# A state-space scan and a bilinear feed-forward: warm-up products cut into narrow ones, and one up unit moved ahead of a pair's scores

## The chip, the cores and the metric

The kernel runs on one core of a Trainium2 chip. The metric is the device time of one execution in microseconds. A core has five engines that run side by side and meet through semaphores: TensorE (PE in the profile; its weight loads are listed apart as PEld), VectorE (DVE), ScalarE (ACT), GpSimd (POOL) and SyncE (SP). DMA transfers are issued from SP, ACT and POOL.

## The reference

The first half is a chunked state-space recurrence per batch (4) and head (8) over 768 tokens with head size 32 and state size 16. The second half multiplies two projections of its result and projects back.

```python
log_a = np.log(np.clip(a, 1e-06, 1.0))
for c in range(nc):                       # chunks of 32 tokens
    cum = np.cumsum(la, axis=-1)
    L = np.exp(cum[:, :, :, None] - cum[:, :, None, :]) * causal
    M = np.einsum('bhin,bhjn->bhij', Cc, Bc) * L
    y_intra = np.einsum('bhij,bhjd->bhid', M, xc)
    y_inter = np.einsum('bhin,bhnd->bhid', Cc, state) * np.exp(cum)[:, :, :, None]
    y[:, :, sl] = y_intra + y_inter
    Bx = np.einsum('bhjn,bhjd->bhjnd', Bc, xc) * decay_from_j[:, :, :, None, None]
    state = decay_full[:, :, None, None] * state + np.sum(Bx, axis=2)
...
x = attn_out.transpose(0, 2, 1, 3).reshape(3072, 256)
out = ((x @ w_a) * (x @ w_b)) @ w_out     # 256 -> 1536 -> 256
```

## The kernel before, in words

The sequence is cut into 6 blocks of 128 tokens. A *pair* is two batches of one block, so there are 12 pairs, two to a block; pairs 0 to 3 have one layout, later pairs another. All instructions stand in an order written out by hand; each engine runs its own in that order.

For a pair the work goes: B and C are scaled by running products of `a` (`scale_bc`), turned so that the state index lies on the partitions (`transposes` or, for later pairs, a transposing DMA, `turn`), multiplied into *scores* (`scores`, lines 428 and 443) in four PSUM banks `SC`, masked causally into SBUF (`mask`: line 483 on DVE; with `by_pool` a copy by ACT, line 480, and the product by POOL, line 481), and multiplied with x (`pv_u`, lines 489 and 503). `ds_mm` (lines 517 and 530) makes the pair's contribution to the state. x of a pair is scaled into `X16` by `scale_x` (line 318 on ACT, line 320 on POOL) or loaded as 16-bit.

The factors for the first two blocks come from PE too: DVE scans `a` (`scan`, line 262), inverts the middle value (`over_mid`) and spreads it (`sel_over_mid`, line 268); `factors_mm` (line 283) turns it with PE into `fps`; DVE's reciprocal (line 834) gives `fB`, and `scale_bc` (line 335) uses both.

The feed-forward of pairs 0 to 3 is made of *up units*. Unit (p, k2) makes two of twelve slices of the hidden layer for pair p: four products with Wa (`aps`, line 680), four with Wb (`bps`), ACT's copy of the first (line 707) and DVE's product of both (line 714). `go(...)` runs units one after the other. Twelve slices done, `out_half` (line 729) multiplies with Wo. From block 2 on both pairs go together (lines 759, 769, 784). `outputs`, called by `group`, makes the y of a block from scores, x and state. Their PSUM banks come from a list of digits, `BANKS`, taken in the order of the calls.

In front, PE has nothing to do until the first factors are there, and short waits after that. `warmup(n, bank, cols)` (line 255) fills them: n products of a zeroed tile with itself, 512 columns wide unless `cols` says otherwise, each with its own weight load, into a bank that nothing reads. They are ordinary instructions of PE's queue: what follows them starts behind them.

Weights are loaded by POOL's software queue in parts: `load_w0(0, 0)` (Wa, first half), `load_w0(1, 0)` and `load_w0(1, 1)` (two halves of Wb's first half), then `load_w`. On POOL these stand between computing instructions.

Of the kernel before, what the change touches and what calls it, by code (L numbers as in the profile page):

```python
# [28 lines left out]
def kernel(  # L29
# [82 lines left out]
    SC = [SC0[:, 0], SC0[:, 1], SC1[:, 0], SC1[:, 1]]  # L112
# [9 lines left out]
    def bank(name):  # L122
        return psf.tile([128, 512], f32, name=name, tag=f"ff{next(banks)}")
# [129 lines left out]
    def warmup(n, bank, cols=512):  # L253
        for _ in range(n):
            nc.tensor.matmul(  # L255
                bank[:, 0:cols], warm[:, 0:128], warm[:, 0:cols], start=True, stop=True, skip_group_check=True
            )


    def scan(lo, hi):  # L260
        for k in range(lo, hi):
            nc.vector.tensor_tensor_scan(Pr[:, k], a_sb[:, k], zero, 1.0, ALU.mult, ALU.add)
# [12 lines left out]
    def factors_mm(lo, hi, fps=None, k0=0):  # L275
        if fps is None:
            fps = bank("fps")
        w = 2 * NBP * H
        F = fps[:, k0 * w : (k0 + hi - lo) * w].rearrange("p (k r c) -> p k r c", k=hi - lo, r=2)
        for k in range(lo, hi):  # L280
            for r in range(2):
                for bt in range(2):
                    nc.tensor.matmul(  # L283
                        F[64 * bt : 64 * bt + 64, k - lo, r],
                        Pr[:, k].rearrange("p (i r) -> p r i", r=2)[:, r],
                        selr[:, k, bt],
                        start=True,
                        stop=True,
                        skip_group_check=True,
                        tile_position=(0, 64 * bt),  # L290
                    )
        return F.rearrange("p k r c -> p (k r c)")
# [14 lines left out]
    def flat(f, lo, hi):  # L307
        return f[:, lo:hi].rearrange("p k r b h -> p (k r b h)")
# [13 lines left out]
    def scale_bc(p, which, eng, factor=None):  # L322
        blk, bp = divmod(p, NBP)
        name, f = (("bm", fB), ("cm", fC))[which]
        raw = by_token(pair_in[p][which]) if p >= P0 else pair_in[p][which].rearrange("p h r n -> p r h n")
        if p >= P0 and which:
            eng.tensor_tensor(
                out=planes[p % 2][:, 4:6].rearrange("p t (h n) -> p t h n", n=N),
                in0=raw,
                in1=of_pair(f, blk, bp).unsqueeze(3).broadcast_to((128, 2, H, N)),  # L330
                op=ALU.mult,
            )
            return
        m_ = mid.tile([128, 2, H, N], f16, name=name, tag=name)
        eng.tensor_tensor(  # L335
            out=m_,
            in0=raw,
            in1=(of_pair(f, blk, bp) if factor is None else factor).unsqueeze(3).broadcast_to((128, 2, H, N)),
            op=ALU.mult,
        )  # L340
        st.setdefault(p, {})[name] = m_
        if p >= P0:
            dst = planes[p % 2][:, 0:4].rearrange("p (t e) (m f n) -> p t e m f n", e=2, f=2, n=N)
            for e in range(2):
                eng.tensor_copy(dst[:, :, e, :, e], m_.rearrange("p t (m f) n -> p t m f n", f=2)[:, :, :, e])
# [44 lines left out]
    def transposes1(which, T_):  # L390
        s = st[1]
        T_ = T_.bitcast(f16)[:, 0:256]
        for r in range(2):
            nc.tensor.transpose(
                T_[:, r * 128 : (r + 1) * 128],
                s[("bm", "cm")[which]][:, r].rearrange("p h n -> p (h n)"),
                ident,
            )
        if which:
            CT = mid.tile([128, 2, Q], f16, name="ct", tag="ct")  # L400
            nc.vector.tensor_copy(
                CT.rearrange("p t (i r) -> p r (t i)", r=2), T_.rearrange("p (r c) -> p r c", r=2)
            )
            s["CT"] = CT
        else:
            BT = mid.tile([128, 2, 2, 2, 64], f16, name="bt", tag="bt")
            s["BT"] = BT

            def part(e):
                nc.scalar.activation(  # L410
                    out=BT[:, e].rearrange("p r t i -> p (r t i)"), in_=T_, func=AF.Copy, scale=par[:, e : e + 1]
                )

            return part
# [7 lines left out]
    def scores(p):  # L422
        BT, CT = st[p]["BT"], st[p]["CT"]
        st[p]["T1"] = mid.tile([128, H, 2, Q], f16, name="t1", tag="t1")
        for e, bt, m in itertools.product(range(2), range(2), range(4)) if p >= P0 else ():
            rows = slice(32 * m, 32 * m + 32)
            c0 = (e * 2 + bt) * Q
            nc.tensor.matmul(  # L428
                SC[m][:, c0 : c0 + Q],
                BT[rows, e, bt],  # L430
                CT[rows, bt],
                start=True,
                stop=True,
                skip_group_check=True,
                tile_position=(32 * m, 0),
            )
        for e in range(2) if p < P0 else ():
            for r in range(2):
                for m in range(4):
                    for bt in range(2):  # L440
                        rows = slice(32 * m, 32 * m + 32)
                        c0 = (e * 2 + r) * Q
                        nc.tensor.matmul(  # L443
                            SC[m][64 * bt : 64 * bt + 64, c0 : c0 + Q],
                            BT[rows, e, r, bt],
                            CT[rows, bt],
                            start=True,
                            stop=True,
                            skip_group_check=True,
                            tile_position=(32 * m, 64 * bt),  # L450
                        )
# [13 lines left out]
    def product0(m2, e):  # L465

        return (
            st[0]["T1"][:, 4 * m2 : 4 * m2 + 4].rearrange("p (m e) r q -> p e m (r q)", e=2)[:, e],
            (SC0, SC1)[m2][:, :, e * 256 : e * 256 + 256],
        )  # L470

    def mask(out_in, by_pool=False, by_token=False):
        o_, i_ = out_in
        if by_token:
            c_ = causal_q.unsqueeze(1).broadcast_to((128, 4, Q))
        else:
            c_ = causal.rearrange("p r q -> p (r q)").unsqueeze(1).broadcast_to((128, 2, 2 * Q))
        if by_pool:
            tmp = mid.tile([128, *c_.shape[1:]], f32, name="tmp", tag="tmp")
            nc.scalar.copy(tmp, i_)  # L480
            nc.gpsimd.tensor_tensor(out=o_, in0=tmp, in1=c_, op=ALU.mult)  # L481
        else:
            nc.vector.tensor_tensor(out=o_, in0=i_, in1=c_, op=ALU.mult)  # L483
# [132 lines left out]
    def evac0(u, bt, eng, py):  # L616
        o_, i_ = X2T[:, 0, bt, u], py[bt][:, u * Q : (u + 1) * Q]
        if eng is nc.scalar:
            nc.scalar.activation(out=o_, in_=i_, func=AF.Copy, scale=YS)
        else:  # L620
            nc.vector.tensor_scalar(o_, i_, YS, None, ALU.mult)
# [96 lines left out]
    def unit(p, k2, between=None):  # L718
        a_ps = unit_mm(p, k2, Wa)
        if between:  # L720
            between()
        b_ps = unit_mm(p, k2, Wb)
        asb = evac_a(a_ps)
        return lambda: times(p, k2, b_ps, asb)
# [20 lines left out]
    def out_half(p, bt):  # L745
        o_ps = bank("ops")
        out_mm(p, bt, o_ps, range(NK))
        out_store(p, bt, o_ps)
# [68 lines left out]
    def go(*items):  # L817
        for p, k2 in items:
            unit(p, k2)()
# [2 lines left out]
        if ("S", p) in st:  # L822
            st[p].update(st.pop(("S", p)))

    warmup(26, SC[3], 128)
    scan(0, 1)
    over_mid(0, 1)
    sel_over_mid(0, 1, nc.vector)
# [3 lines left out]
    fps = bank("fps")  # L832
    v = factors_mm(0, 1, fps)
    nc.vector.reciprocal(flat(fB, 0, 1), v)
    warmup(1, SC[3])
    v1 = factors_mm(1, 2, bank("fps"))
    warmup(1, SC[3])
    scale_bc(0, 0, nc.vector)
    scale_bc(0, 1, nc.vector, v.rearrange("p (r b h) -> p r b h", r=2, b=NBP)[:, :, 0])
    scan(3, 4)  # L840
    tb, tcp = bank("tb"), bank("tc")
# [1 line left out]
    nc.scalar.copy(flat(fC, 0, 1), v)  # L843
    nc.scalar.copy(flat(fC, 1, 2), v1)
    scan(4, 5)
    warmup(1, SC[3])
    warmup(2, SC[3], 128)
    scores(0)
    scale_bc(1, 0, nc.gpsimd)
    mask(product0(0, 0))  # L850
# [1 line left out]
    mask(product0(1, 1), by_pool=True)  # L852
    scale_bc(1, 1, nc.vector)
    mask(product0(1, 0))
    warmup(3, tcp)
    part = transposes1(0, bank("tb"))
    part(0)
    part(1)
    warmup(2, tcp)
    py = [bank("py0"), bank("py1")]  # L860
    pv_u(0, 0, py, True)
    ds_mm(0, 256, py)
    transposes1(1, SC[0])
    for bt in range(2):
        evac0(0, bt, nc.scalar, py)
    warmup(1, tcp)
    pv_u(0, 1, py, True)
    for bt in range(2):
        evac0(1, bt, nc.scalar, py)
# [181 lines left out]
    prep(6)  # L1051
    masked(4, (0, 1, 2))
    out_half(2, 0)
    go((3, 0), (3, 1), (3, 2))
    scores(5)
    mask(product(5, 3), by_pool=True, by_token=True)
    prep_x(4)
# [3 lines left out]
    loads_bc(8)  # L1061
    masked(5, (0, 1, 2))
    out_half(2, 1)
    go((3, 3), (3, 4))
    scale_x(5, nc.scalar)
    go((3, 5))
    group(2)
# [92 lines left out]
```

## Time and profile before

| | |
|---|---|
| runs shown | 121.36, 121.40, 122.35 us; median 121.40 |
| profiled execution: time, span | 122.31 us, 120.6 us |
| PE busy | 114.6 us, 95% of the span |
| DVE, ACT, POOL busy | 87.2, 72.7, 62.3 us |
| warm-up products | 29 of 128 columns and 9 of 512, from 1.25 to 10.1 us |
| first product with factors (line 283) starts | 4.13 us |
| scores of pair 5 (line 428) start | 41.44 us |
| outputs of block 2, product with x (line 489) start | 46.05 us |

The times of a chain or timeline count from the span's start. A timeline line gives start, length, engine, line, operation, tile written and tiles read, shape and how many; in brackets the engine's idle time ahead of it and what ended it. In the chain of work that ended last, each piece is what held up the next; "issue" is time in which the engine waited for nothing that the profile shows.

### The profile page before, as it was taken

Reading aid. Unit: us, or ns where it says so; the run is one execution under the profiler, and the core shown is the slowest. Engines: PE = TensorE matmul, PEld = TensorE weight load, DVE = VectorE, ACT = ScalarE, POOL = GpSimd, SP = SyncE. Lnnn points to the kernel's source line nnn. Section 1 sums busy time; section 2 is a strip of 40 time slices with the busy share of each in tenths; the row PEclk is TensorE's granted clock in tenths of the full one; section 3 lists DMA queues with packets and bytes.
Section 4 is the critical chain, followed back from the end, with each engine's and each line's share of the span. In section 5 each row is a group of like instructions: output and inputs, shape, how many; then the busy total and the mean of one; then the engine's idle time right before and its main releaser. Section 6 shows DMA issues by size and latency. Waiting matters only on the chain.

```text
span 120.6 us, 3713 instructions
## 1 busy us (share of the span) xinstructions
PE 114.6 (95%) x1454; PEld 80.5 (67%) x1454; DVE 87.2 (72%) x171; ACT 72.7 (60%) x148; POOL 62.3 (52%) x109
## 2 busy tenths in 40 slices
PE   5998699999999999999999999999999999999990
PEld 5745499888898898645476464766464684655890
DVE  5989695995989888499984999677899445847100
ACT  0477557685965767787667737645646737566220
POOL 6998998299985686199912992249200000000200
PEclk9999999999999999999999999999999999999999
DMA  3999999997879999699588954879301012010032
GB/s 62 128 173 163 177 208 168 236 159 72 82 107 94 151 112 143 111 131 159 56 147 121 247 184 98 88 109 192 134 0 49 2 43 85 0 49 0 20 110 87
DMA packets 69185, 13.44 MB, mean 111 GB/s; under 512 B 64048, under 2 KB 68912, under 8 KB 69168
## 3 DMA queue, kind: packets, MB, share of 16 engines
q1 hardware_dynamic: 62272, 9.31, 47.5%
q0 software_dynamic: 4368, 3.54, 18.2%
q10 hardware_dynamic: 2528, 0.36, 2.1%
q8 instruction: 11, 0.18, 0.6%
q14 instruction: 6, 0.05, 0.1%
HBM read 11.11 MB, written 3.15 MB: 118 GB/s over the span
## 4 chain that ended last, share of the span: by engine, by line
PE 93%; DVE 3%; issue 1%; ACT 0%
PE ops L784 18%; PE aps L759 18%; PE bps L759 17%; PE ops L729 9%; PE bps L680 9%; PE aps L680 8%; PE SC L255 3%; PE SC L428 2%; PE SC L489 2%; PE SC L443 1%; DVE t L483 1%; PE SC L503 1%; PE aps L695 1%; PE SC L579 1%; PE fps L283 1%
## 5 line engine op out<-in xcount | busy, mean ns | idle before, releaser
L707 ACT COPY asb<-aps 128x512 f32<-128x512 f32 x72 | 41.6, 587 | 13.3 <-PE aps L759 9.6
L769 DVE TENSOR_TENSOR hkb<-bps,asb 128x512 f16<-128x512 f32 x48 | 32.3, 689 | 12.7 <-ACT asb L707 11.6
L759 PE MATMUL aps<-XB,Wa 128*128 128x512 f16 x96 | 28.6, 379 | 0.0
L759 PE MATMUL bps<-XB,Wb 128*128 128x512 f16 x96 | 28.5, 379 | 0.0
L784 PE MATMUL ops<-Wo,hkb 128*128 128x256 f16 (+1 forms) x204 | 22.5, 267 | 0.0
L784 PEld LDWEIGHTS <-hkb 128*128 128x128 f16 x204 | 18.5, 98 | 3.1
L483 DVE TENSOR_TENSOR t<-SC,causal_q 128x512 f16<-128x512 f32 x27 | 17.2, 682 | 3.3 <-PE SC L428 3.3
L714 DVE TENSOR_TENSOR hk<-bps,asb 128x512 f16<-128x512 f32 x24 | 16.1, 684 | 3.1 <-PE bps L680 1.2
L759 PEld LDWEIGHTS <-Wb 128*128 128x128 f16 x96 | 9.9, 103 | 10.9
L759 PEld LDWEIGHTS <-Wa 128*128 128x128 f16 x96 | 9.7, 103 | 9.1 <-issue 0.2
L798 POOL DMA_DIRECT2D out_dram<-osb x1 | 0.6, 642 | 27.9 <-ACT osb L796 27.9
L796 ACT ACTIVATE osb<-ops 128x256 f32<-128x256 f32 (+1 forms) x16 | 6.0, 377 | 14.3 <-PE ops L784 14.2
L680 PE MATMUL bps<-X2T,Wb 128*128 128x256 f16 x96 | 13.8, 273 | 0.0
L680 PE MATMUL aps<-X2T,Wa 128*128 128x256 f16 x88 | 12.7, 273 | 0.0
L729 PE MATMUL ops<-Wo,hk 128*128 128x256 f16 x96 | 11.5, 273 | 0.0
L481 POOL TENSOR_TENSOR t<-tmp,causal_q 128x512 f16<-128x512 f32 x5 | 5.8, 1159 | 10.0 <-ACT tmp L480 9.9
L680 PEld LDWEIGHTS <-Wb 128*128 128x128 f16 x96 | 9.8, 103 | 0.7
L729 PEld LDWEIGHTS <-hk 128*128 128x128 f16 x96 | 8.9, 98 | 1.4
L680 PEld LDWEIGHTS <-Wa 128*128 128x128 f16 x88 | 8.9, 103 | 0.6
L320 POOL TENSOR_SCALAR x<-xn 128x512 f16<-128x512 f32 x6 | 8.9, 1491 | 0.6
L483 DVE TENSOR_TENSOR t<-SC,causal 128x512 f16<-128x512 f32 x12 | 7.7, 683 | 0.8 <-PE SC L443 0.7
L335 POOL TENSOR_TENSOR bm<-bn,fB 128x256 f16<-128x256 f32 x11 | 6.9, 623 | 2.5 <-DMA bn<-in_B_dram 2.3
(115 smaller groups left out, 127.8 us busy)
## 6 DMA issues: line engine op xcount, KB each, us to landing
out_dram<-osb SPq DMA_DIRECT2D x22, 128.0 KB, 1.8
xn<-in_x_dram SPq DMA_DIRECT2D x6, 256.0 KB, 4.3
cn<-in_C_dram SPq DMA_DIRECT2D x8, 128.0 KB, 3.9
bn<-in_B_dram SPq DMA_DIRECT2D x8, 128.0 KB, 4.5
Wa<-in_moe_w_a_dram POOLq DMA_DIRECT2D x2, 384.0 KB, 6.4
Wo<-in_moe_w_out_dram POOLq DMA_DIRECT2D x2, 384.0 KB, 5.5
xn<-in_x_dram SPq DMA_DIRECT2D x4, 128.0 KB, 3.7
Wb<-in_moe_w_b_dram POOLq DMA_DIRECT2D x2, 192.0 KB, 6.1
```

The lines of the kernel that those rows point to most:

```text
L320: eng.tensor_scalar(xo, xi, XS, None, ALU.mult)
L335: eng.tensor_tensor(out=m_, in0=raw, in1=(of_pair(f, blk, bp) if factor is None else factor).unsqueeze(3).broadcast_to((128, 2, H, N)), op ...
L481: nc.gpsimd.tensor_tensor(out=o_, in0=tmp, in1=c_, op=ALU.mult)
L483: nc.vector.tensor_tensor(out=o_, in0=i_, in1=c_, op=ALU.mult)
L680: nc.tensor.matmul(ps[:, kk * 2 * Q : (kk + 1) * 2 * Q], w_of(W, k, f), X2T[:, p, :, f], start=(f == 0), stop=(f == 1), skip_group_check=True,
L707: (nc.vector.tensor_copy if on_dve else nc.scalar.copy)(asb, a_ps)
L714: nc.vector.tensor_tensor(out=s["hk"][:, 2 * k2 : 2 * k2 + 2, :].rearrange("p k q -> p (k q)"), in0=b_ps, in1=asb, op=ALU.mult)
L729: nc.tensor.matmul(o_ps[:, 0:d_model], hk[:, k, bt * Q : (bt + 1) * Q], Wo[:, k, :], start=(k == 0), stop=(k == NK - 1), skip_group_check= ...
L759: nc.tensor.matmul(t_, w_of(W, k, f), XB[:, blk - P0 // NBP, f].rearrange("p t j q -> p (t j q)"), start=(f == 0), stop=(f == 1), skip_gro ...
L769: return lambda: nc.vector.tensor_tensor(out=s["hk"][:, k], in0=ps[1], in1=asb, op=ALU.mult)
L784: nc.tensor.matmul(o_ps[:, 0:w], hk[:, k, c * Q : (c + 1) * Q], Wo[:, k, cs], start=(k == 0), stop=(k == NK - 1), skip_group_check=True,)
L796: nc.scalar.activation(out=o_sb[:, 0:w], in_=o_ps[:, 0:w], func=AF.Copy, scale=1.0 / (YS * YS))
```

## The change

The first call of `warmup` makes 34 narrow products in place of 26. Every later one of 512 columns is replaced by four of 128: the two between the factors' products, the one ahead of pair 0's scores, the three and the two around the transposes of pair 1, and the one ahead of `pv_u(0, 1)`. That makes 35 more products with 35 more weight loads, all ahead of the first up unit. Later, up unit (3, 3) moves ahead of the scores of pair 5, past `prep_x(4)`, `loads_x(6)`, `prep(7)`, `loads_x(7)`, `loads_bc(8)`, the masks of pair 5 and `out_half(2, 1)`. The list of banks stays, so unit (3, 3) now takes banks 1 and 3 and `out_half(2, 1)` takes bank 2, where they had 3 and 2, and 1.

```diff
-    warmup(26, SC[3], 128)
+    warmup(34, SC[3], 128)
     scan(0, 1)
...
     nc.vector.reciprocal(flat(fB, 0, 1), v)
-    warmup(1, SC[3])
+    warmup(4, SC[3], 128)
     v1 = factors_mm(1, 2, bank("fps"))
-    warmup(1, SC[3])
+    warmup(4, SC[3], 128)
     scale_bc(0, 0, nc.vector)
...
     scan(4, 5)
-    warmup(1, SC[3])
-    warmup(2, SC[3], 128)
+    warmup(6, SC[3], 128)
     scores(0)
...
     mask(product0(1, 0))
-    warmup(3, tcp)
+    warmup(12, tcp, 128)
     part = transposes1(0, bank("tb"))
     part(0)
     part(1)
-    warmup(2, tcp)
+    warmup(8, tcp, 128)
     py = [bank("py0"), bank("py1")]
     pv_u(0, 0, py, True)
     ds_mm(0, 256, py)
     transposes1(1, SC[0])
     for bt in range(2):
         evac0(0, bt, nc.scalar, py)
-    warmup(1, tcp)
+    warmup(4, tcp, 128)
     pv_u(0, 1, py, True)
...
     out_half(2, 0)
-    go((3, 0), (3, 1), (3, 2))
+    go((3, 0), (3, 1), (3, 2), (3, 3))
     scores(5)
     mask(product(5, 3), by_pool=True, by_token=True)
     prep_x(4)
...
     masked(5, (0, 1, 2))
     out_half(2, 1)
-    go((3, 3), (3, 4))
+    go((3, 4))
     scale_x(5, nc.scalar)
```

## The prediction

> **What bounds the kernel now.** I read the engine shares first, then the chain that ended last in order of time, then the engines' timelines in the two stretches that the change touches.
>
> ```profile
> PE 114.6 (95%) x1454; PEld 80.5 (67%) x1454; DVE 87.2 (72%) x171; ACT 72.7 (60%) x148; POOL 62.3 (52%) x109
> ...
> q8 instruction: 11, 0.18, 0.6%
> ...
> PE 93%; DVE 3%; issue 1%; ACT 0%
> ```
>
> TensorE (PE) carries 93% of the chain. From 14.77 us on the chain is PE work without a gap worth naming up to the last output, so a microsecond that PE loses anywhere is a microsecond at the end. All that can be won or hidden lies in the first 14.77 us:
>
> ```profile
> 1.25 2.95 PE SC L255 x26
> 4.21 0.54 PE fps L283 x8
> 4.75 0.54 PE SC L255
> 5.29 0.37 PE fps L283 x8
> ...
> 6.82 0.60 PE SC L443 x32
> ...
> 13.06 0.34 PE SC L503 x30
> 13.40 1.08 issue
> 14.48 0.21 PE SC L503
> 14.77 0.83 PE bps L680 x6
> ```
>
> The first product that the kernel needs, the factors of line 283, stands directly behind the 26 warm-up products: no wait lies between. Its operand had been ready on VectorE (DVE) since 3.54 + 0.18 = 3.72 us, and DVE then waits for it:
>
> ```profile
> 3.54 0.18 DVE L268 TENSOR_TENSOR selr<-sel,rmid 32x32 f32<-32x32 f32 x1
> ...
> 4.79 0.36 DVE L834 RECIPROCAL fB<-fps 128x32 f32<-128x32 f32 x1 [0.16 <-PE fps L283]
> 5.18 0.42 DVE L335 TENSOR_TENSOR bm<-bn,fB 128x256 f16<-128x256 f32 x1
> ```
>
> The second place is "issue" at 13.40: PE stands for 1.08 us in the middle of the 32 products of line 503, with no semaphore to wait for. The DMA records name a cause: queue q8, kind "instruction", moves 11 packets of 16 KB, one for about every 250 rows of PE (a row is a weight load or a product), so it is PE's code. The first runs from 12.28 to 13.23 us and PE goes on at 14.48, after 449 rows. I take it that the code ran out there.
>
> **The change, part by part.**
>
> *Wide into narrow.* Nine products of 512 columns become 36 of 128. The price per column is the same, by the starts in the trace: while the clock is still slow a narrow one follows the last after 0.107 us (26 in a row) and a wide one takes 0.43; later narrow ones (and the transposes of line 357, each with a weight load of its own) come every 0.055 us and wide ones every 0.216. Four narrow are 0.43 and 0.22 us, so nothing. What hides it if that is wrong: all of them but the first 34 stand ahead of a wait for DVE or POOL. The tightest is after the scores of pair 0: 12 narrow, two transposes, 8 narrow are 22 x 0.055 = 1.2 us, and the masks that the next products wait for come 1.4 us after these scores. That cover is 0.2 us.
>
> ```profile
> L255 PEld LDWEIGHTS <-warm x38: 95/147/147, 1.2 to 9.7; 128*128 128x128 f16 x38
> L255 PE MATMUL SC<-warm x32: 219/311/607, 1.3 to 6.4; 128*128 128x128 f16 x29, 128*128 128x512 f16 x3
> ```
>
> [...] The trace shows 55 ns and 216 here.
>
> *Eight more at the head.* They come before anything is due, and at the slow rate: 8 x 0.107 = 0.85 us. The clock opens at 5.31 us in the trace's clock record (the 512-column product at 4.68 lasts 607 ns, the one at 5.58 390), so the first factors, now at 4.13 + 0.85 = 4.98, run their second half faster: I take 0.1 off, 0.75. Bounds: all eight at the fast rate 0.44, all slow 0.85. What is late next: the reciprocal (4.79 to 5.54), bm, cm, the transposes, ct, the scores (6.82 to 7.57), the masks, all one dependency after the other on DVE, PE and ScalarE (ACT); the scan between them fills DVE but is shorter than the waits. On POOL the scaling of pair 1 (7.41, behind DMA issues that do not move) stays; the mask after it waits for the scores and moves by 0.7, and with it the issue of the second half of Wb's first part, 9.21 to 9.9. Its landing at 14.72 stays: the software queue is still moving the loads issued before it until 12.7, with the engines full.
>
> *What of the 0.75 is left at 14.77.* In this profile PE stands from 13.40 to 14.48 anyway, so a plain delay would vanish in it. But the 35 added products are 70 rows of code. If the code ends after 449 rows as before, that is now 70 rows earlier in the work: in the third of the six products of line 680 that began at 12.24, with five products and nearly all of line 503 still to do. PE gets there at 12.35 + 0.75 = 13.1 and stands until the code comes. If that is at 14.48 again (the packet waited on full DMA engines, whose traffic does not depend on PE), 5 x 0.109 + 0.2 for line 503 + 0.28 up to line 680 give 15.5 for 14.76: +0.75. Bounds: the request moves with the row that causes it; those rows are now about 1.0 us earlier (the row 256 before the stop ran at 8.80; now at 7.03 + 0.75), so the code is there at 13.5, PE comes to line 680 at 14.5 and waits for the landing at 14.72: nothing to +0.25. In the other direction the request comes later by the front's 0.6: +1.35. I take +0.75; the first packet started 3.5 us after the row 256 rows before the stop, the second only 2.2, which says that full DMA engines and not the row set it.
>
> *The up unit of pair 3.* Two evacuations, one product and 8 matmuls change places with the scores of pair 5; the work is the same, the scores come 4 x 2 x 0.109 = 0.87 us later, and with them ACT's copy and POOL's mask, behind which X of pair 4 is scaled:
>
> ```profile
> 42.63 1.16 POOL L481 TENSOR_TENSOR t<-tmp,causal_q 128x512 f16<-128x512 f32 x1 [1.46 <-ACT tmp L480]
> 43.88 1.50 POOL L320 TENSOR_SCALAR x<-xn 128x512 f16<-128x512 f32 x1
> ...
> 46.05 0.63 PE L489 MATMUL SC<-t,x 128*32 128x128 f16 x32
> ```
>
> That scaling ends at 45.38 and is wanted at 46.05: slack 0.67. It will end at 46.25, so PE waits 0.2, with the hop 0.25. Bounds 0 and 0.3. DVE's three masks end at 45.1 (44.21 before) and free the scores' banks for 45.81: hidden by 0.7; without that cover, their rest would be added. The banks of the products rotate in another order, but each one's last reader ends ahead of its next writer by 0.3 us or more. Behind on POOL stands the preparation of pair 7: its bm waits for a landing at 46.54 anyway, so its turn on SP's queue (47.89) and the loads of X of pair 7 and of pair 8's inputs behind it move by 0.3; the scores of pair 7 want them at 54.3. Nothing there.
>
> **The sum.** +0.75 + 0.25 = +1.0 us. The profiled execution has a span of 120.6 and a time of 122.31, so it becomes 123.3. The runs shown are 121.36, 121.40 and 122.35: the profiled one is like the third, 0.9 over the median. I add the sum to the median and round up a little, because a run without the stop at 13.40 has nothing to absorb the delay: 122.5 (own range 122.0 to 123.2).
>
> **The rivals.**
>
> *The stop is new or longer* (0.16). The quick runs may be those whose code comes in time, 0.9 us faster. Then 70 rows more make them stand too: 0.9 + 0.75 + 0.25 = +1.9, 123.3. For it: the two levels of times differ by about the stop. Against: one profile, and nothing that shows a quick run.
>
> *Narrow products come no faster than their weight loads* (0.08). The load's row says 95 to 98 ns in the fast state. At that rate the 22 take 2.1 us, 0.7 past the cover: +1.7, 123.1. Against: four in a row at 55 ns. [...]
>
> *The stop swallows the delay* (0.13). The code request moves up with its row, PE meets the landing of Wb at 14.72: +0 to 0.25, with pair 3's 0.25 +0.4: 121.8.
>
> *The stop disappears: no loss* (0.10). Place: 13.40. If the code is asked for so much earlier that it is there by 13.1, and the half of Wb without that packet in its way lands by 14.4 (its other fifteen engines were done at 13.57), PE reaches line 680 at 13.40 + 0.28 + 0.75 = 14.43 for 14.76: -0.33 + 0.25 = -0.1, 121.3. It decides from a resumption before 13.1, 1.4 earlier than now; the row moves by 1.0 only. If X of pair 4 is in time too, -0.3. More than 1% faster would need the eight products hidden, and the chain shows nothing that hides them.
>
> **How the numbers follow.** One per cent, 1.2 us, is about what a measurement of this kernel tells from no change. The forecast has 0.53: its upper part, over 122.6, is half, 0.26. With the two slower rivals, 0.24, slower has 0.50. Same has the forecast's lower half and the swallowed and vanished ones but for 0.07 that I leave for faster: 0.43. The range goes from the swallowed case's lower end, 121.5, to the new stop's upper end, 123.5.
>
> **What would show it.** Right: 34 narrow products at 0.107 us, line 283 at about 5.0, the reciprocal at 5.55, scores near 7.6; an idle "issue" of 1 us or more inside line 680 or its neighbours near 13.1 and none in line 503; line 680's second half of Wb at 15.5; line 489 at 46.3 counted from the same shift, behind POOL's line 320. Wrong: line 283 before 4.8, a gap that has gone, or line 680 at 14.8.

## The result and the profile after

The changed kernel takes 123.25 us (median of 21 runs, 122.59 to 124.67); the kernel before, in the same study, 122.43 (21 runs, 121.36 to 123.71). The ratio is 1.009, with an interval of 1.0066 to 1.0114. Measured once more, beside the second group of experiments (e8 below), it was 1.004 (1.0004 to 1.0076). So the change costs about 0.5 to 1.1 us by the two ratios. The ratios leave out executions that took over 1.5% more than the fastest of their kernel, and the medians and means here do not, so the two can differ by a few tenths of a per cent. The profiled execution took 124.22 us with a span of 122.5, 1.9 more than the one before; that is a worse draw than the median.

The page after, in the lines that answer to those of before (engine shares; code packets; the chain's shares):

```profile
PE 116.9 (95%) x1489; PEld 83.9 (68%) x1489; DVE 87.1 (71%) x171; ACT 72.7 (59%) x148; POOL 62.4 (51%) x109
...
q8 instruction: 11, 0.18, 0.6%
...
PE 73%; POOL 6%; DVE 5%; DMA 4%; SPq 4%; issue 3%; ACT 1%; POOLq 0%; DVEq 0%; ACTq 0%
```

PE has 35 products more. Its share of the chain has fallen from 93% to 73%: the end is now set in part by POOL, by a load (`cn<-in_C_dram`) and by SP's queue, which before were nowhere in it. The chain's head, in order of time:

```profile
1.25 3.81 PE SC L255 x34
5.06 0.54 PE fps L283 x8
5.60 0.54 PE SC L255 x4
...
8.39 0.66 PE SC L443 x20
...
14.03 0.66 PE bps L680 x6
14.69 0.35 PE SC L503 x32
```

Line 283 starts 0.85 us later, four narrow products take 0.54 us where one wide one took 0.54, and all 32 products of line 503 run in one piece: the "issue" of 1.08 us is gone. Here are the longest waits of PE over the whole span, after (in us, times, longest):

```profile
PE SC L255 <- DVE warm L202: 1.2, 1, 1.2
PE SC L503 <- POOL t L481: 1.0, 1, 1.0
PE SC L394 <- DVE cm L335: 0.2, 1, 0.2
PE SC L489 <- POOL x L320: 0.2, 1, 0.2
```

The second line is new. It is not in the front: it is pair 3, at 35.6 to 36.6 us, and the timeline of POOL shows where it comes from (the bracket is the idle time ahead and what ended it):

```profile
32.92 0.62 POOL L327 TENSOR_TENSOR planes<-cn,fC 128x256 f16<-128x256 f32 x1 [1.60 <-DMA cn<-in_C_dram]
33.50 0.62 POOL L335 TENSOR_TENSOR bm<-bn,fB 128x256 f16<-128x256 f32 x1
...
35.39 1.15 POOL L481 TENSOR_TENSOR t<-tmp,causal 128x512 f16<-128x512 f32 x1
```

POOL stands 1.60 us for pair 4's C. Behind that in its queue is `mask(product(3, 3))`, line 481, and PE's line 503 needs it: 35.26 + 0.35 us of work, then 0.98 idle up to 36.59. In the first profile of before, the same preparation began at 30.40 without a wait, the mask stood ready in time, and line 503 ran in one piece:

```profile
30.40 0.62 POOL L327 TENSOR_TENSOR planes<-cn,fC 128x256 f16<-128x256 f32 x1
...
32.88 1.16 POOL L481 TENSOR_TENSOR t<-tmp,causal 128x512 f16<-128x512 f32 x1
```

```profile
34.70 0.42 PE L503 MATMUL SC<-t,x 64*32 64x128 f16 x32
```

### The profile page after: what moved, and what is told of

Its sections match the earlier page's. It is cut to its first block, busy times and chain, and to the rows that moved or that the text cites. A ratio compares the mean times of both kernels' runs of the same rounds, so it can differ in the third digit from the quotient of the medians.

```text
span 122.5 us, 3783 instructions
## 1 busy us (share of the span) xinstructions
PE 116.9 (95%) x1489; PEld 83.9 (68%) x1489; DVE 87.1 (71%) x171; ACT 72.7 (59%) x148; POOL 62.4 (51%) x109
## 4 chain that ended last, share of the span: by engine, by line
PE 73%; POOL 6%; DVE 5%; DMA 4%; SPq 4%; issue 3%; ACT 1%; POOLq 0%; DVEq 0%; ACTq 0%
PE ops L784 18%; PE aps L759 17%; PE bps L759 17%; PE SC L255 5%; DMA cn<-in_C_dram 4%; SPq L143 4%; PE aps L680 4%; PE bps L680 3%; DVE t L483 3%; PE ops L729 2%; PE SC L489 2%; POOL t L481 2%; PE SC L428 2%; DVE hk L714 1%; POOL x L320 1%
## 5 line engine op out<-in xcount | busy, mean ns | idle before, releaser
L327 POOL TENSOR_TENSOR planes<-cn,fC 128x256 f16<-128x256 f32 x8 | 5.0, 621 | 7.3 <-DMA cn<-in_C_dram 7.3
```

## How the profiles are compared

Every experiment was timed and one execution of it profiled. From the scores of pair 6 (49.46 us before) on all profiles run alike within 0.02 us, so the differences in span can be split by the start times of a few products. For each profile these are set against the first profile of before, and the growth between one and the next is written down. *Front*: up to line 695. *Stop*: from there to the seventh product of line 680 with Wb (14.76 us before), where the code stop and the landing of Wb lie. *Pair 2*: to its scores (23.64); where it grows, PE waits for POOL's cm in line 357, and in m3, e6, e8 and m2 for Wb's next part in line 680 as well. *Pair 3*: to the scores of pair 4 (37.07), where the new wait lies. *Unit*: from line 579 to line 489 (46.05). *Pair 6*: to its scores (49.46), which wait for `turned` (in e5, by the profile, for ACT's copy of line 741). The rest is below 0.03 except 0.37 in n3, before the scores of pair 5. "Clock" is the time at which the clock record shows TensorE's full clock (e8 and m2 have no such entry; there the spacing of the warm-up products falls from 0.107 to 0.056 us at 4.6 and at 9.9 us); "rows" is the number of PE instructions (weight loads and products) that stand ahead of the first up unit more than before.

| profile | rows | clock | front | stop | pair 2 | pair 3 | unit | pair 6 | span |
|---|---|---|---|---|---|---|---|---|---|
| before, first | 0 | 5.31 | 0 | 0 | 0 | 0 | 0 | 0 | 120.61 |
| before, second (n4) | 0 | 5.29 | +0.12 | -0.93 | 0.00 | +0.04 | 0.00 | +1.03 | 120.85 |
| e3 unit alone | 0 | 8.89 | +0.77 | -0.27 | 0.00 | 0.00 | +0.25 | 0.00 | 121.35 |
| e2 eight alone | 16 | 5.85 | +0.78 | -0.39 | 0.00 | +0.21 | 0.00 | +0.34 | 121.54 |
| e7 eight and unit | 16 | 4.51 | +0.38 | -0.98 | 0.00 | 0.00 | +0.25 | 0.00 | 120.27 |
| m3 tiny eight | 16 | 9.63 | +1.09 | -1.27 | +0.70 | 0.00 | 0.00 | +0.40 | 121.50 |
| n3 tiny eight, loads early | 16 | 10.17 | +1.23 | -1.07 | +0.03 | 0.00 | 0.00 | +0.86 | 122.02 |
| n1 few rows | 22 | 5.36 | +0.72 | -0.91 | +0.32 | 0.00 | +0.25 | +0.35 | 121.32 |
| e1 narrow alone | 54 | 9.91 | +0.94 | -1.26 | +0.22 | +1.03 | 0.00 | +0.81 | 122.33 |
| e6 narrow and unit | 54 | 9.90 | +0.94 | -1.12 | +0.64 | +0.36 | +0.25 | 0.00 | 121.66 |
| e5 front | 70 | 4.21 | +0.24 | -0.93 | +0.20 | +0.39 | 0.00 | +0.50 | 120.99 |
| after, first | 70 | 9.82 | +1.63 | -1.27 | +0.20 | +1.11 | +0.25 | 0.00 | 122.52 |
| after, again (e8) | 70 | none shown | +0.42 | -0.80 | +0.50 | +0.71 | +0.25 | 0.00 | 121.68 |
| m1 rows, wide products | 70 | 4.71 | +0.57 | -0.76 | 0.00 | 0.00 | +0.25 | 0.00 | 120.67 |
| n2 the same again | 70 | 9.95 | +1.81 | -1.27 | +0.20 | +0.77 | +0.25 | 0.00 | 122.36 |
| e4 weights early | 70 | 10.03 | +2.06 | -1.26 | +0.17 | +0.64 | +0.25 | 0.00 | 122.45 |
| m4 loads early | 70 | 6.02 | +0.83 | -0.74 | 0.00 | 0.00 | +0.25 | 0.00 | 120.93 |
| m2 mask first | 70 | none shown | +1.63 | -1.27 | +0.70 | +1.42 | +0.25 | +0.33 | 123.64 |

Two things are plain before any single experiment. The times of one and the same kernel scatter by over 2 us (before: 121.4 to 123.7 in 21 runs), and a profile is one draw from that: the clock opens anywhere from 4.2 to 10.2 us. And the gains and losses are small waits in several places, not one delay that is carried through.

## Experiments

The theory first held against the result was the prediction's own (a delay of the front, carried through a stop that stays). The first group takes the change apart; "means" below are means of all timed runs, minus those of before in the same study, each with a standard error of about 0.25 us.

### Narrowing alone (e1)

Every call of 512 columns as in the change; the first warm-up keeps its 26 products.

```diff
-    warmup(1, SC[3])
+    warmup(4, SC[3], 128)
...
-    warmup(3, tcp)
+    warmup(12, tcp, 128)
...
```

> The narrowing alone: 26 products at the head, nine wide ones become 36 narrow, units in the old order. Theory 1 (the loss is made by the eight more at the head, which make POOL issue the weight loads late, and by the unit's move): the same within 0.3%, line 283 at 4.1 us, no wait of PE in line 503 of pair 3. Theory 2 (narrow products let TensorE's clock open later, 9.8 us in place of 5.3): most of the loss, 0.6 to 0.9%, the clock's opening after 8 us, the first scores 0.5 us or more late.

Measured: 122.68 us, ratio 0.9989 (0.9947 to 1.0031). Line 283 starts at 4.13 us as before, which it must, since nothing ahead of it was narrowed; between the two factors four narrow products took the time of the wide one. The stop is gone; the wait in pair 3 is there, 0.91 us.

### Eight more alone, wide products kept (e2)

```diff
-    warmup(26, SC[3], 128)
+    warmup(34, SC[3], 128)
```

> Eight more narrow products at the head alone, the wide ones stay. Theory 1: line 283 at 5.0, POOL's weight loads (line 176) issued 0.8 us or more late, pair 4's C landing late, PE waits 0.5 to 1 us in line 503 of pair 3 for POOL's mask: 0.5 to 0.8% slower. Theory 2: within 0.3%, since the delay goes into the stop at 13.4 us.

Measured: 122.92 us, ratio 0.998 (0.9939 to 1.0022). The front is 0.78 later and 0.39 of that is given back where the stop was: PE waits 0.81 for Wb's landing instead of 1.08 for code. In pair 3, POOL waits 0.80 us for pair 4's B, whose last parts land together at 32.2 us, and PE waits 0.09 for t.

### The unit's move alone (e3)

```diff
-    go((3, 0), (3, 1), (3, 2))
+    go((3, 0), (3, 1), (3, 2), (3, 3))
     scores(5)
...
-    go((3, 3), (3, 4))
+    go((3, 4))
```

> The unit's move alone. Both theories: PE waits 0.2 us ahead of line 489 for POOL's scaling of x of pair 4 (line 320), 0.25 us in all, 0.2% slower; the front as before. If the move is neutral, that wait is missing.

Measured: 122.72 us, ratio 0.9968 (0.9926 to 1.0011). The 0.25 us before line 489 is there, and in every profile with the move, and in none without. The stop is there too; PE's timeline:

```profile
13.77 0.41 PE L503 MATMUL SC<-t,x 64*32 64x128 f16 x30
15.04 0.23 PE L503 MATMUL SC<-t,x 64*32 64x128 f16 x2 [0.87 <-issue]
```

The front is 0.77 late although nothing in it differs from before: its clock opened at 8.89 us. So a clock can open late without narrow products.

### Weights issued earlier in the changed kernel (e4)

A rival for pair 3: POOL issues the weights later because its queue waits for a mask (10.84 us for 9.21), SP's loads behind them come later, and so does pair 4's C.

```diff
     scale_bc(1, 0, nc.gpsimd)
     mask(product0(0, 0))
     mask(product0(0, 1))
+    load_w0(1, 1)
+    w1 = load_w(1)
     mask(product0(1, 1), by_pool=True)
...
-    load_w0(1, 1)
-    w1 = load_w(1)
```

> The changed kernel, with the issues of Wb's second half, and of the second halves of Wa and Wb, ahead of POOL's mask of pair 0 in place of behind it. Theory 1: weights issued near 8 us, SP's loads of pair 3 start by 18.8 as in the kernel before, C of pair 4 lands by 30.5, the wait of 1 us in line 503 of pair 3 is gone: 0.1 to 0.4% over before. Theory 2: as the changed kernel, 0.9% over before.

Measured: 123.63 us, ratio 1.0072 (1.0029 to 1.0114). The weights are issued at 7.95 to 9.39 us and pair 3's B at 17.72 (20.01 in the changed kernel, 18.75 before), but pair 4's B still lands at 33.27 and PE still waits 0.36 us. Late weights are not the cause, at most a part of its size. Nor does the time at which the load is issued decide it: pair 4's C left at 22.66 us here, with a wait of 0.36 us, and at 27.03 in e2, with 0.09.

### The front of the change, without the unit's move (e5)

The edits of e1 and e2 together, which is all of the change but the unit:

```diff
-    warmup(26, SC[3], 128)
+    warmup(34, SC[3], 128)
...
-    warmup(1, SC[3])
+    warmup(4, SC[3], 128)
...
```

> The whole front of the changed kernel, units in the old order. If the parts simply add (theory 1): the eight carry it, 0.5 to 0.8% over before, no wait ahead of line 489. If the front's delay goes into the stop for code (theory 2): within 0.3% of before.

Measured: 122.98 us, ratio 1.002 (0.9981 to 1.0059). With the clock open at 4.21 us the 70 rows delay line 695 by 0.24 only. The wait in pair 3 stays, 0.26 us: it doesn't need a late front. And a short stop is left, in line 680:

```profile
12.48 0.27 PE L680 MATMUL bps<-X2T,Wb 128*128 128x256 f16 x1
12.94 0.71 PE L680 MATMUL bps<-X2T,Wb 128*128 128x256 f16 x5 [0.18 <-issue]
```

It stands behind 222 products and 223 weight loads, as the stops in line 503 of before and e3 do: 70 rows more in front have moved it to an instruction 70 rows earlier in the work.

### Narrowing and the unit; eight and the unit; the change again (e6, e7, e8)

e6 has the edits of e1 and e3, e7 those of e2 and e3, e8 is the changed kernel as it is. Against the changed kernel that is, for e6 and for e7 in turn:

```diff
-    warmup(34, SC[3], 128)
+    warmup(26, SC[3], 128)
```

```diff
-    warmup(4, SC[3], 128)
+    warmup(1, SC[3])
...
```

> The changed kernel with 26 products at the head. Theory 1: 0.2% over before, the wait of 0.2 us ahead of line 489, line 283 at 4.1. Theory 2 (the narrow ones and their code carry the loss): 0.6% or more.

> Eight more and the unit's move, wide products kept. Theory 1: as the changed kernel, 0.7 to 1.0% over before. Theory 2: 0.2%, the unit's move alone.

> The changed kernel once more, beside the same runs of before as the three parts. 0.7 to 1.1% over before. If TensorE's clock opens by chance early or late (it opened at 5.3, 5.9 and 8.9 us in runs with wide products, at 9.8 to 10.0 in three with narrow ones), this look may open at another time; if the narrow products hold it back, it opens after 9.5 again.

Measured: e6 122.87 us, 1.0043 (0.9999 to 1.0087); e7 123.06, 1.0022 (0.9983 to 1.0061); e8 123.38, 1.004 (1.0004 to 1.0076). The wait in pair 3: 0.24, none, 0.59 us. With all eight combinations the means can be averaged: with the eight minus without, +0.3 us; narrowing +0.3; the unit +0.15, each with a standard error of some 0.15 to 0.2. That they add up to the change's +0.8 fits several small costs; it doesn't prove any one of them.

Up to here the wait in pair 3 stood in all six profiles with the narrowing, 0.24 to 0.98 us, and in none of the four without it was it over 0.09. What differs at that place is a transfer. The landings of pair 4's B come in sixteen parts; in the six, fifteen are done and one is over a microsecond late, and the 16 KB code packet (queue q8) runs at that time. In the changed kernel the packet runs at 30.79 to 31.75 us, B's fifteenth part lands at 31.95 and the last at 33.34; in the first profile of before the packet comes at 32.06, after B's landing at 30.45. The packets follow the rows, plainest where they are far apart: the seventh and eighth begin after 1717 and 1973 rows before and after 1714 and 1977 in the changed kernel. So more rows ahead bring them earlier in the work.

### Wide products, and as many rows (m1, n2)

If rows do it, 70 rows without a narrow product must do it as well. Against the kernel before:

```diff
+    def tiny(n):
+        for _ in range(n):
+            nc.tensor.matmul(
+                SC[3][0:32, 0:32], warm[:, 0:32], warm[:, 0:32], start=True, stop=True, skip_group_check=True
+            )
+
+    tiny(35)
     warmup(26, SC[3], 128)
...
-    go((3, 0), (3, 1), (3, 2))
+    go((3, 0), (3, 1), (3, 2), (3, 3))
...
```

> The unit's move as in the change, but the wide products stay wide; instead of the narrowing and the eight more, 35 tiny products (32 weights x 32 columns) run at the very start: 70 more instructions in TensorE's stream, as in the change, at about the same time. Theory of the shifted code packets: the stop at row 449 is gone, the fourth 16 KB instruction packet runs at 29.5 to 31.5 us (before 32.06), pair 4's C and B land with a last engine 1 us or more behind, and PE waits 0.2 to 1.0 us for t of line 481 before line 503 of pair 3, with not one product narrowed: ratio 1.004 to 1.008. Theory that the narrow form itself makes that wait (other clock, other times of the front): packets as in the kernels with wide products or the wait absent, ratio 0.998 to 1.002.

> The kernel of wide products with 35 tiny ones ahead, once more. If the collision of the code packet with pair 4's landing is a matter of rows and of chance within it, a second look has a landing whose last engine is 1 us late and a wait before line 503 of pair 3; if wide products are spared, there is none, as in the first look. Ratio as before, 1.002 to 1.008.

Measured: m1 123.43 us, ratio 1.0043 (1.0007 to 1.0078); n2, the same kernel, 123.63, 1.0095 (1.0057 to 1.0133). The 35 cost about what the eight did: line 283 at 4.98 us in m1, 5.18 in n2. The first profile missed the expectation: packet at 29.45 us, B's last part only 0.25 us behind the others, no wait; the clock opened early in it, at 4.71 us, and C was issued at 25.36. The second, with the clock at 9.95 and C at 27.69, has it, packet at 30.58, B's last part 0.92 us behind at 33.18. PE and POOL in n2:

```profile
35.44 0.35 PE L503 MATMUL SC<-t,x 64*32 64x128 f16 x20
36.44 0.29 PE L503 MATMUL SC<-t,x 64*32 64x128 f16 x12 [0.64 <-POOL t L481]
```

```profile
33.34 0.62 POOL L335 TENSOR_TENSOR bm<-bn,fB 128x256 f16<-128x256 f32 x1 [1.19 <-DMA bn<-in_B_dram]
...
35.23 1.16 POOL L481 TENSOR_TENSOR t<-tmp,causal 128x512 f16<-128x512 f32 x1
```

So the narrow form is not needed for this wait, and with the rows it is frequent and not certain. In m1 the stop of the front is again left, 0.33 us at 13.42, in line 680 behind 222 products.

### Narrow products, and few rows (n1)

The counterpart: the first warm-up's columns in wide products, everything else as changed, 22 rows more than before in place of 70.

```diff
-    warmup(34, SC[3], 128)
+    warmup(8, SC[3])
+    warmup(2, SC[3], 128)
```

> The changed kernel, but its first warm-up of 34 narrow products is issued as 8 wide and 2 narrow ones: the same columns, 48 instructions less in TensorE's stream, so 22 more than before in place of 70; the other 38 narrow products and the unit's move stay. If the number of instructions ahead places the fourth code packet on pair 4's landing, it runs after it here (at 31 us or later), the last engine of B's landing is at most 0.3 us late, and PE doesn't wait for t before line 503 of pair 3: ratio 1.000 to 1.005. If the narrow form does it some other way, the wait of 0.25 to 1 us is there: ratio 1.004 to 1.010. Either way the stop at row 449 is gone and the unit costs 0.25 us before line 489.

Measured: 123.31 us, ratio 1.0082 (1.0038 to 1.0126). The fourth packet is back at 32.66 us, B lands whole at 31.17, and the wait in pair 3 is gone with 38 products still narrow:

```profile
34.83 0.42 PE L503 MATMUL SC<-t,x 64*32 64x128 f16 x32
```

```profile
31.33 0.62 POOL L335 TENSOR_TENSOR bm<-bn,fB 128x256 f16<-128x256 f32 x1 [0.18 <-DMA bn<-in_B_dram]
...
33.22 1.16 POOL L481 TENSOR_TENSOR t<-tmp,causal 128x512 f16<-128x512 f32 x1
```

The landing and the wait came out as expected. The time did not: the ratio is above the range given. In the profile, 0.25 us of the 0.71 is the unit, 0.35 a wait of pair 6, 0.32 lies in pair 2, and front and stop together give 0.19 back. Taking the wait in pair 3 away by this edit did not make the kernel measurably faster.

### Pair 4's loads earlier in the changed kernel (m4)

```diff
-    loads_x(3, nc.sync)
     loads_bc(4)
+    loads_x(3, nc.sync)
```

> The changed kernel, but SP issues pair 4's C and B ahead of pair 3's x, whose values are needed later. Theory that pair 4's landing collides with the code packet at 29.4 to 31.8 us: C and B are issued 1 to 4 us earlier, land before the packet, POOL's line 335 of pair 4 begins earlier and the wait before line 503 of pair 3 falls below 0.1 us; ratio 1.002 to 1.005. Theory that POOL is late for its own work (state sums, masks), not for the landing: wait unchanged, 0.25 to 1 us, ratio 1.006 to 1.010.

Measured: 123.03 us, ratio 1.0024 (0.9987 to 1.006). C is issued at 22.32 us (27.55 in the changed kernel), POOL's bm of pair 4 begins at 31.06 instead of 33.50, and the wait before line 503 is gone. Of the versions that keep all rows and the unit's move (the changed kernel, e4, m2, m4) this has the lowest ratio; its profile has 0.32 us left over before, 0.25 of it the unit's. It is not faster than before. Its front has a stop as well:

```profile
13.71 0.71 PE L680 MATMUL bps<-X2T,Wb 128*128 128x256 f16 x5 [0.36 <-issue]
```

### POOL's mask ahead of pair 4's preparation (m2)

```diff
 scores(3)
+mask(product(3, 3), by_pool=True)
 prep(4, (2,))
-mask(product(3, 3), by_pool=True)
```

> The changed kernel, but POOL's mask of pair 3 stands ahead of pair 4's preparation in POOL's queue. Theory of POOL's queue: the wait before line 503 of pair 3 is gone even though pair 4's C and B land late, the time falls by 0.25 to 0.6 us against the changed kernel, ratio 1.001 to 1.005; line 418 (turn of pair 4) starts at most 0.5 us later than it did and nothing waits for it. Theory that the loss sits in the front (a later clock, a later line 695): the wait goes but the scores of pair 4 and 5 are no earlier, ratio 1.007 to 1.010.

Measured: 125.06 us, ratio 1.0146 (1.0104 to 1.0188): a miss, 2 us over before. The wait before line 503 is gone, but POOL now sits out line 480 first (mask at 33.24 us) and begins the preparation of pair 4 at 34.36 where the changed kernel did at 32.92; its turn comes later and PE waits there instead:

```profile
PE SC L428 <- DMA turned<-planes: 1.6, 2, 1.4
```

POOL's queue is tight on both sides of this mask. Moving the mask ahead trades the wait in pair 3 for a larger one; an earlier landing (m4) takes it away.

### Sixteen rows more and nothing else; with the loads early as well (m3, n3)

These ask whether the saving at the stop can be had for less than it costs.

Against the kernel before, with `tiny` as above; n3 has m4's edit besides.

```diff
+    tiny(8)
     warmup(26, SC[3], 128)
```

> The kernel before with 8 tiny products (32x32, 16 more instructions) ahead of the first warm-up and nothing else. Theory that the stop is a matter of where the code packet is asked for: the stop of 1.08 us at row 449 is gone as with the eight products of 128 columns, the tiny products cost 0.1 to 0.4 us, no wait in pair 3: 0.3 to 0.9 us faster than before, ratio 0.993 to 0.998. Rival, that the stop is only moved or that the time of the front and not the rows takes it away: stop of 0.5 to 1.1 us still there, ratio 1.000 to 1.003.

> The kernel before with 8 tiny products (32x32) ahead of the first warm-up, and pair 4's C and B issued ahead of pair 3's x. If what the change pays is the landing of pair 4 and what it saves is the stop, this has the saving without the price: no stop, no wait in pair 3, no wait before line 489, 0.2 to 0.8 us faster than before, ratio 0.993 to 0.998. If both are small beside the time at which the clock opens, ratio 0.998 to 1.002.

Measured: m3 122.82 us, ratio 0.9994 (0.9959 to 1.0028); n3 123.14, 1.0052 (1.0012 to 1.0092). The stop is gone in both, and neither is faster. Both profiles have a late clock (9.63 and 10.17 us) and a front 1.09 and 1.23 us late, which eats most of the saving. n3 has waits for `turned` of 0.31 us in pair 5, the 0.37 left out of the table's columns, and 0.80 in pair 6 (its span is 122.02). In it the fourth packet (32.69 to 33.76 us) runs beside pair 5's C and B, whose last parts land 1.46 and 1.29 us behind the others; whether that makes the wait in pair 5 was not followed. No version that was run beats the kernel before beyond its interval.

### A second profile of the kernel before (n4)

> The kernel before once more, for its profile alone. If the stop belongs to the place of row 449 in the code, it is there again with 0.8 to 1.1 us, wherever the clock opens; if the first look had it by chance, TensorE waits there less than 0.3 us. The fourth code packet runs after 31.5 us and there is no wait in pair 3.

Measured: 122.55 us, span 120.9. PE's timeline at the place of the stop:

```profile
13.11 0.55 PE L503 MATMUL SC<-t,x 64*32 64x128 f16 x32
...
13.95 0.73 PE L680 MATMUL bps<-X2T,Wb 128*128 128x256 f16 x5 [0.23 <-DMA Wb<-in_moe_w_b_dram]
```

No stop. The first code packet ran from 11.06 us here and from 12.28 in the first profile. The front is within 0.12 us of that one, so the stop of 1.08 us is a matter of when the packet came, not of the row alone. In all five profiles with a stop (before, e3, e5, m1, m4) it stands at the same row, and PE goes on 1.25 to 1.59 us after the packet's end; where the packet ends early enough, there is none. This execution has lost the same microsecond elsewhere, in a wait that the first one had not:

```profile
PE SC L428 <- DMA turned<-planes: 1.0, 1, 1.0
```

## Why the prediction was right or wrong

*The sum.* +1.0 us was forecast; +0.8 by the medians of the first study and +0.6 in the second were measured. The total is near, but by luck: its main term is wrong and others took its place. The time itself, 122.5 us, stood on the median of the three runs shown, 121.40; the 21 runs of before have 122.43, without the two levels that the prediction took from the three. So the base alone was 1.0 us low.

*Wide into narrow costs nothing in PE's time*: right. At the slow clock four take 0.54 us between the factors as the wide one did. With the clock open the narrow products of e5 and e8 start every 0.056 us, and those of the first profile after too, from 9.83 us on. But 27 of the 35 new products, and with them 54 of the 70 rows, come from this step, and the prediction priced the rows at the first packet alone.

*Eight more, +0.85 at line 283 and 0.75 behind it*: right at line 283 (4.99 us). Behind it the size is the clock's. At line 695 the delay is 0.72 to 0.83 us in e2, n1 and m4, which opened at 5.36 to 6.02 us, near the prediction's 5.31: there the 0.75 is right. It is +0.24 and +0.42 at line 695 where it opened earlier (e5 at 4.21, e8 at about 4.6), and +1.63 where it opened at 9.82 us. The prediction took the opening at 5.31 us for a property of the kernel. The record has it between 4.21 and 10.17, late in some narrow kernels (not in e5, e8, n1 and m4), in e3 whose front is that of before, and in wide ones (m3, n2, n3).

*The stop stays, PE goes on at 14.48 us again, and the delay is passed on (+0.75)*: this is the step that failed. The place was right: the code runs out after the same number of rows (222 products and 223 weight loads, 445 for the prediction's 449), and e5, m1 and m4 stop in line 680 at 12.94, 13.42 and 13.71 us, where the prediction had put it, with none in line 503. The time was wrong: these stops last 0.18, 0.33 and 0.36 us in place of 1 us or more, and the seven other profiles with 54 or 70 rows added, the first one after among them, have none. The argument was that full DMA engines set the packet's time, so that it would come no earlier. With rows added, few or many, it began at 10.46 to 11.47 us in all fifteen profiles, and at 12.28, 12.73 and 11.06 in the three without (before, e3, n4). So the second half of Wb in line 680 starts at 15.12 us in the first profile after and at 14.38 in e8, for 15.5 forecast, and the front's delay and what is given back at the stop nearly cancel: +1.63 - 1.27 and +0.42 - 0.80. That is nearest to the rival "the stop disappears". What sets the time of the first packet stays open: 16 rows brought it as early as 70, and without any it was once early too. A feature of one profile was priced as if each run had it.

*The unit's move, +0.25*: right to the hundredth. Line 320 and line 489 after:

```profile
45.17 1.16 POOL L481 TENSOR_TENSOR t<-tmp,causal_q 128x512 f16<-128x512 f32 x1 [2.34 <-ACT tmp L480]
46.42 1.50 POOL L320 TENSOR_SCALAR x<-xn 128x512 f16<-128x512 f32 x1
```

```profile
47.98 0.52 PE L489 MATMUL SC<-t,x 128*32 128x128 f16 x24 [0.18 <-POOL x L320]
```

"Nothing there" behind it on SP's queue was too short, to the good: the loss ahead of pair 6's scores is 0.34 to 1.03 us in six of the seven profiles without the move and 0.33 and 0.35 in two of the eleven with it. That would make the move a small gain on balance, which e3's ratio allows. Why the move spares pair 6 was not tried.

*A chain that is PE alone from 14.77 us on*: true of that profile, and the reason why the largest loss of the first profile after, 1.11 us in pair 3, was not seen: this is a term that the sum does not have. POOL had some 0.9 us of slack in pair 3: its mask ended at 34.04 us (32.88 + 1.16), and the products of line 503 ran from 34.70 to 34.95, the last twelve of which need it. A landing 1 to 2 us late uses that up. The prediction looked for who waits behind each moved instruction. It had seen the first packet stand in the way of one part of Wb's load, but it did not ask where the ten later packets would fall. The count of rows goes with the wait: seven of the eight profiles with 54 or 70 rows more (and POOL's and SP's order from pair 3 on unchanged) have it, 0.24 to 0.98 us, and of the eight with 0 to 22 (n3, with its loads early, among them) none has more than 0.09. The clock does not: e5 and e8 opened early and have the wait, e3, m3 and n3 opened late and have none. Nor does the narrow form: n2 has the wait with wide products, n1 has none with 38 narrow ones, one profile each. That a packet holds up one part of a load shows beyond pair 4. Over the loads of inputs and weights issued before 36 us in all 18 profiles, the last part lands more than 0.8 us behind the fifteenth in 78 of 272 where a code packet ran within the two microseconds before the fifteenth landed, and in 13 of 333 where none did. That the packet occupies the one engine whose part comes late is inferred from the times: the records don't name the engine of a transfer.

Two losses stood beside code packets here: where one came late (the first of before, 12.28 to 13.23 us) PE stood for 1.08 us, and one in time (the fourth of the first profile after, 30.79 to 31.75) still ran beside a load whose last part landed at 33.34 us, 1.39 behind the fifteenth.

*What stays open.* How much of the 0.8 us is pair 3's wait and how much the other places can't be settled at this scatter: n1 has no such wait in its profile and was timed no faster than the change. m4 was timed at 1.0024, which speaks for the wait, but its interval and that of e8 overlap. Whether the added rows change how often the clock opens late can't be told from so few profiles.

## What to carry to other kernels

An instruction that costs its engine no time still has weight. Here PE's 2908 rows came with eleven transfers of 16 KB, about one for every 264, and 70 rows more in front shifted the later ones against the loads: the fourth began at 30.79 us in the first profile after, for 32.06 before, and ran beside pair 4's B. When a stall in one profile has no semaphore behind it, look at a second profile of the same kernel before pricing it; here it was there in one of two. Runs of the same program with a few rows more can then show whether it stays at its row. And where a queue such as POOL's takes work for two pairs in turn, an operand of one pair can stand behind a load of the other: look at that slack too, and not only at the busiest engine's.

## What was not expected of the hardware

The full clock came at 4.2 to 10.2 us after the span's start, for kernels whose line 283 starts within 1.1 us of each other, and at 4.71 and 9.95 us in two runs of one kernel (m1, n2). In the first profile after, the record's 9.82 us is where the warm-up products change from one every 0.107 us to one every 0.056. The late opening came with about 1.2 us at line 695 (+1.63, against +0.42 for the same changed kernel in e8, which opened at about 4.6). What sets the time of the opening no run shows.

A code packet of 16 KB took 0.9 to 1.6 us. In the seven profiles with the wait in pair 3, the last of the sixteen parts of B's load of 128 KB, which ran beside the packet, came 0.9 to 1.4 us behind the rest, and that of C's 1.85 in the first profile after.

PE's stop for code stands behind 222 products and 223 weight loads in all five profiles that have one, at two different instructions of the work. That it waits for code is inferred from the times: no semaphore stands there, and PE goes on 1.25 to 1.59 us after the first packet's end.
